# First loads and first steps laid in another order, in a windowed attention with FFN on one core

## The chip, the cores and the metric

One core of a Trainium2 chip runs the whole program. The metric is device time in microseconds, the median of several executions; the profile is of one execution and gives a span, from the first to the last instruction, which is a little less than the device time. Engines: TensorE (PE; its weight loads are PEld), VectorE (DVE), ScalarE (ACT), GpSimd (POOL) and SyncE (SP). Each works through its own queue in the order in which the program wrote it.

## The reference, cut to what matters

Batch 4, 8 heads, 768 tokens, head size 64; n_global is 8, n_local 96. A token attends to the first 8 tokens and to the 96 tokens up to itself.

```python
scores = scale * np.matmul(q, k.transpose(0, 1, 3, 2))
rel = pos[:, None] - pos[None, :]
is_global = pos[None, :] < int(n_global)
is_local = (rel >= 0) & (rel < int(n_local))
keep = is_global | is_local
dist = np.where(is_global & ~is_local, float(n_local), np.abs(rel).astype(np.float32))
scores = np.where(keep, scores - slopes[:, None, None] * dist[None], -1e9)   # softmax over the last axis
x = (softmax(scores) @ v).transpose(0, 2, 1, 3).reshape(3072, 512)
h = x @ w_in                                        # 512 x 2048
g = np.maximum(h, 0.0) + np.log1p(np.exp(-np.abs(h)))
return g @ w_out                                    # 2048 x 512, float32
```

## The kernel before, in words

The 3072 tokens are 24 blocks of 128, six to a batch. With a window of 96, a block needs the scores against itself and the block ahead of it; the 8 global tokens are copied into unused rows of the block ahead (`gk` for keys, `gv` for values). The FFN works on chunks of two blocks, 256 tokens. The heads go in two halves of four, written n.0 and n.1.

The program is a list of named steps, each a short function. Steps with a block number n:

- `l`, `lv`: loads of q and k, and of v, issued by GpSimd (line 97), 128 KB each on arrival. `load_w_in` (line 102) and `load_w_out` (line 108) bring the weights in four pieces each, 512 KB a piece.
- `t`: eight transposes on TensorE into the bank `tr` (line 208), first those of q, then those of k; VectorE copies them to QT (line 214) and KT (line 220). From block 8 on `d` does it by DMA from SP. The openings of blocks 0 and 1 have `tr_first_q` and `tr_first_k`, where k goes to a bank of its own and ScalarE copies KT of block 1.
- `s`: scores of a half, 8 matmuls (4 for the first block of a batch) into the one bank s_ps (line 258); VectorE adds the bias and gives Z (lines 270 and 272), and with it s_ps is free.
- `e`: the exponential of Z on ScalarE, giving Pb (line 294).
- `p`: Pb times v on TensorE into the one bank x_ps (line 307); VectorE takes the reciprocal of the sum (line 318) and multiplies, giving xsf (line 321).
- `x`: transposes of xsf on TensorE through the bank `tr` (line 336), copied to XT (line 339); from block 6 on by DMA.

Steps with a unit number u, eight units to a chunk: `f` is FFN in, 8 matmuls of 256 columns into one of two buffers hT (line 352), then two passes of ScalarE, an exponential (e_sb, line 357) and a logarithm (G, line 358). `o` is FFN out, 4 matmuls of 512 columns (line 372), and with every fourth a copy on VectorE and a store. Units f0 and f1 need the first piece of w_in, f2 and f3 the second, f4 and f5 the third, f6 and f7 the fourth; o0 and o4 need the first piece of w_out, o1 and o5 the second, and so on. `g` makes GpSimd wait for a G, so that later loads come when they should. `w` is a warm matmul of 512 columns on zeros, into a buffer nobody reads (line 452).

Each engine's queue is the program's order, so a step that waits holds up what stands behind it on its engine. The order comes from three places: the loads written out at the top (lines 151 to 156 and 176 to 179), the function `opening` (line 464), which handles blocks 0 and 1 with 28 warm matmuls in between, and the string `ORDER` (line 420), which goes from f0 to f27. What is not named there is sorted by due times (lines 510 to 521). Loads by GpSimd use eight semaphores in turn: a load waits until the eighth load ahead of it has landed.

Of the kernel before, what the change touches and what calls it, by code (L numbers as in the profile page):

```python
# [19 lines left out]
def kernel(  # L20
# [11 lines left out]
    nc = tc.nc  # L32
# [18 lines left out]
    NU = NFB // 2  # L51
    NWC = 4
# [23 lines left out]
    q_t = [q_r[n % RQK] for n in range(NB)]  # L76
    k_t = [k_r[n % RQK] for n in range(NB)]
    v_t = [v_r[n % RV] for n in range(NB)]
# [3 lines left out]
    q_f = const.tile([P, H, D], F32, name="q_f")  # L82
    k_f = const.tile([P, H, D], F32, name="k_f")
# [11 lines left out]
    def load(n, src, dst):  # L95
        b, i = divmod(n, BPB)
        nc.gpsimd.dma_start(  # L97
            dst[n][:, :, 0:D], src[b, :, i * P : (i + 1) * P, :].rearrange("h s d -> s h d")
        )

    def load_w_in(c):
        nc.gpsimd.dma_start(
            w_in_c[c][:],
            moe_w_in[:, c * FW : (c + 1) * FW].rearrange("(m p) f -> p m f", p=P),
        )

    def load_w_out(c):
        nc.gpsimd.dma_start(
            w_out_c[c][:],
            moe_w_out[c * FW : (c + 1) * FW, :].rearrange("(a p) c -> p a c", p=P),  # L110
        )

    def load_qk(n):
        load(n, q, q_t)
        load(n, k, k_t)

    def load_v(n):
        load(n, v, v_t)

    def load_block(n):  # L120
        load_qk(n)
        load_v(n)

    _tables = list(get_activation_tables(nc.m.arch).keys())
    nc.scalar.add_instruction(
        mybir.InstLoadActFuncSet(
            name=nc.get_next_instruction_name(),
# [20 lines left out]
        allow_small_or_imprecise_dtypes=True,  # L148
    )
    make_identity(nc, ident)  # L150
    load(1, q, q_t)
    load(1, k, k_t)
    load(0, v, v_t)
    load(1, v, v_t)
    load_w_in(0)
    load_w_in(1)

    def tables():
        nc.vector.tensor_scalar(
# [13 lines left out]
    tables()  # L173
    ones(2, RV)

    load_block(2)
    load_block(3)
    load_w_in(2)
    load_w_in(3)

    def head_of(half, r):
        return 4 * half + 2 * ((r // 2) % 2) + r // 4

    def bias_first(half):
        for r in range(0, 8, 2):
            nc.scalar.mul(bias0[:, half, r // 2, :], dist_0[:], -slopes[head_of(half, r)])

    def bias_rest(half):
        for r in range(8):
            nc.scalar.mul(  # L190
                biasA[:, half, r, :], (dist_p if r % 2 else dist_d)[:], -slopes[head_of(half, r)]
            )
# [73 lines left out]
    def add_bias(n, half):  # L266

        Z = new_Z(n, half)
        if n == first_of(n):
            nc.vector.tensor_tensor(Z[:, 0:4, :], s_ps[:, 0:8:2, :], bias0[:, half, :, :], ALU.add)  # L270
        else:
            nc.vector.tensor_tensor(Z[:], s_ps[:], biasA[:, half, :, :], ALU.add)  # L272

    def sc(n, half):

        qk(n, half, lambda r: s_ps[:, r, :])
        if n < NBT:
            add_bias(n, half)
            return
        s_lo = ps.tile([P, 4, P], F32, tag="tr", name="s_lo")  # L280
        s_hi = ps.tile([P, 4, P], F32, tag="o2", name="s_hi")
        qk(n, 1, lambda r: (s_lo if r < 4 else s_hi)[:, r % 4, :])
        add_bias(n, 0)
        step, bias = (2, bias0) if n == first_of(n) else (1, biasA)
        w = 4 // step
        Z = new_Z(n, 1)
        for i, s_i in enumerate((s_lo, s_hi)):
            regs = slice(i * w, i * w + w)
            nc.vector.tensor_tensor(Z[:, regs, :], s_i[:, 0:4:step, :], bias[:, 1, regs, :], ALU.add)  # L289

    def ex(n, half):
        nreg = 4 if n == first_of(n) else 8
        Pb = work.tile([P, 8, P], BF16, tag="Pb", name="Pb")
        nc.scalar.activation(  # L294
            Pb[:, 0:nreg, :], Zt.pop((n, half))[:, 0:nreg, :], AF.Exp, scale=inv_sqrt
        )
        Pt[n, half] = Pb

    def pv(n, half):
        first = n == first_of(n)  # L300
        Pb = Pt.pop((n, half))
        for lh in range(4):
            mm, sub = lh // 2, lh % 2
            h = 4 * half + lh
            for t in range(1 if first else 2):
                r = 2 * sub + mm if first else 4 * sub + 2 * mm + t
                nc.tensor.matmul(  # L307
                    x_ps[:, lh, :], Pb[:, r, :], v_t[n - t][:, h, :],
                    start=(t == 0), stop=(t == 1 or first),
                )  # L310
        if half == 0:
            xt[n] = (
                work.tile([P, H, D], BF16, tag="xsf", name="xsf"),
                work.tile([P, H], F32, tag="rcp", name="rcp"),
            )
        xsf, rcp = xt[n]
        h0 = 4 * half
        nc.vector.reciprocal(  # L318
            rcp[:, h0 : h0 + 4], x_ps[:, :, D : D + 1].rearrange("p h e -> p (h e)")
        )  # L320
        nc.vector.tensor_tensor(  # L321
            xsf[:, h0 : h0 + 4, :], x_ps[:, :, 0:D],
            rcp[:, h0 : h0 + 4][:, :, None].to_broadcast([P, 4, D]), ALU.mult,
        )

    def tr_x(n):
        xsf, _ = xt.pop(n)
        if n % 2 == 0:
            XT[n // 2] = xtp.tile([P, NPAIR, CT], BF16, tag="XT", name="XT")
        dst = XT[n // 2][:, :, P * (n % 2) : P * (n % 2) + P]  # L330
        if n >= NDX:
            nc.sync.dma_start_transpose(dst, xsf[:].rearrange("p h d -> p (h d)"))
            return
        tr = ps.tile([P, 2, NPAIR, P], BF16, tag="tr", name="tr")
        for m in range(NPAIR):
            nc.tensor.transpose(  # L336
                tr[:, 0, m, :], xsf[:, 2 * m : 2 * m + 2, :].rearrange("p a b -> p (a b)"), ident[:]
            )
        nc.vector.tensor_copy(dst, tr[:, 0, :, :])
# [66 lines left out]
    def gate(s):  # L406
# [3 lines left out]


    LAG = 13
    KINDS = {
        "t": tr_qk, "d": dma_qk, "gk": gk, "gv": gv, "s": sc, "e": ex, "p": pv, "x": tr_x,
        "l": load_qk, "lv": load_v, "g": gate,
    }

    ORDER = """  # L420
        f0 gv2 gk2 t2 l6 lv6 f1 s2.0 e2.0 f2 t3 l7 lv7 s2.1 e2.1 gk3 f3 p2.0 s3.0 e3.0 f4 p2.1
        gv3 s3.1 e3.1 gk4 f5 x2 p3.0 f6 t4 p3.1 f7 x3 s4.0 f8 f9 e4.0 s4.1 t5 f10 g9 l8 gk5 e4.1
        f11 gv4 o4 p4.0 o0 o1 s5.0 f12 p4.1 o5 o6 e5.0 x4 gv5 s5.1 e5.1 f13 p5.0 o2 t6 o7 p5.1
        s6.0 e6.0 o3 t7 f14 g13 l9 s6.1 d8 p6.0 e6.1 f15 x5 s7.0 o8 o9 p6.1 e7.0 s7.1 gk8 f16
        g15 lv8 d9 p7.0 x6 e7.1 o10 f17 f18 g17 l10 p7.1 f19 s8.0 x7 d10 f20 g19 lv9 e8.0 gv8
        gk9 o11 e8.1 f21 f22 g21 l11 p8.0 s9.0 o12 p8.1 o13 e9.0 gv9 o14 e9.1 f23 p9.0 f24 f25
        p9.1 x8 f26 x9 gk10 gv10 o15 f27
    """

    def steady(n):  # L430
# [5 lines left out]
            f"x{n}": s + 3.25,  # L436
        }

    def run(name):
        kind = name.rstrip("0123456789.")  # L440
        nums = [int(i) for i in name[len(kind):].split(".")]
        if kind in "fo":
            (ffn1 if kind == "f" else ffn2)(*divmod(nums[0], NU))
        else:
            KINDS[kind](*nums)

    warm_ps = ps2.tile([P, DM], F32, tag="hT", name="warm_ps")

    def warm(count):

        for _ in range(count):
            nc.tensor.matmul(warm_ps[:], warm_in[:, 0:P], warm_in[:])  # L452

    def tr_first_q(n):
        tr = qk_bank()
        tr_in(tr, 0, q_t[n])
        to_QT(n, tr)

    def tr_first_k(n):
        tr = ps.tile([P, 2, NPAIR, P], BF16, tag="o2", name="tr_k")  # L460
        tr_in(tr, 1, k_t[n])
        to_KT(n, tr, nc.vector.tensor_copy if n == 0 else nc.scalar.copy)

    def opening():

        warm(8)
        bias_first(0)
        bias_first(1)
        bias_rest(0)
        bias_rest(1)  # L470
        nc.vector.tensor_copy(q_t[0][:], q_f[:])
        nc.vector.tensor_copy(k_t[0][:], k_f[:])
        tr_first_q(0)
        warm(1)
        tr_first_k(0)
        warm(2)
        sc(0, 0)
        ex(0, 0)
        tr_first_q(1)
        tr_first_k(1)  # L480
        warm(1)
        sc(0, 1)
        ex(0, 1)
        warm(1)
        pv(0, 0)
        sc(1, 0)
        ex(1, 0)
        warm(1)
        pv(0, 1)
        warm(2)  # L490
        sc(1, 1)
        tr_x(0)
        ex(1, 1)
        warm(3)
        pv(1, 0)
        warm(5)
        pv(1, 1)
        warm(3)
        tr_x(1)
        warm(1)  # L500

    opening()
    load_block(4)
    load_block(5)
    for c in range(NWC):
        load_w_out(c)
    first_steps = ORDER.split()
    for name in first_steps:
        run(name)
# [47 lines left out]
```

## Time and profile before

| what | value |
|---|---|
| median of 3 runs | 218.59 us (218.58 to 220.5) |
| profiled execution, its own time | 218.55 us |
| its span | 216.8 us |
| TensorE busy | 210.1 us, 97% |
| ScalarE busy | 163.2 us, 75% |
| VectorE busy | 116.1 us, 54% |
| GpSimd busy | 74.0 us, 34% |
| software DMA queue, share of 16 engines | 83.8% |
| first FFN matmul (f0) | 15.86 us |

The page shows busy times and shares of the span per engine, and groups of instructions by line. A timeline line gives the start, the length, the engine, the line of the program, what is written from what, how many instructions went together, and in brackets how long the engine was idle before and what released it. TensorE's matmuls are pipelined: the length of one includes the time until its result is there, so what a step costs TensorE is read from start to start.

### The profile page before, as it was taken

The numbers are of one execution on the slowest core, as the hardware profiler recorded it, in microseconds if no ns is written. First come the engines' busy times: TensorE is split into PE (matmuls) and PEld (weight loads), VectorE is DVE, ScalarE is ACT, GpSimd is POOL, SyncE is SP. The second block draws the span as 40 slices with busy tenths as digits, with TensorE's granted clock in tenths as the row PEclk, the third lists the DMA queues.
The fourth block names the chain that finished last, engine by engine and source line by source line (L and its number), as shares of the span: only waits on it lengthen the run. The fifth ranks groups of instructions, "written<-read, shape, count | busy, mean of one in ns | idle before, by whom it ended". The sixth has DMA issues, their size and how long they took to land.

```text
span 216.8 us, 5048 instructions
## 1 busy us (share of the span) xinstructions
PE 210.1 (97%) x2004; PEld 142.3 (66%) x2004; DVE 116.1 (54%) x259; ACT 163.2 (75%) x266; POOL 74.0 (34%) x117
## 2 busy tenths in 40 slices
PE   7989899999999999999999999999999999999993
PEld 2448776666768666666677666667667667666453
DVE  6776965696674464464674674364574573011121
ACT  7737998567999979768878878868978978777200
POOL 8959473331534624424334334343311000000000
PEclk9999999999999999999999999999999999999999
DMA  9999999999999999999999999999992620111112
GB/s 129 162 178 187 172 193 206 165 161 136 124 96 168 142 167 155 136 153 102 153 102 135 152 117 124 155 146 91 170 136 41 97 73 15 60 51 48 48 48 97
DMA packets 110071, 27.06 MB, mean 125 GB/s; under 512 B 102624, under 2 KB 107104, under 8 KB 110048
## 3 DMA queue, kind: packets, MB, share of 16 engines
q0 software_dynamic: 77024, 13.37, 83.8%
q1 hardware_dynamic: 33024, 13.38, 31.8%
q8 instruction: 15, 0.25, 0.4%
q14 instruction: 8, 0.07, 0.1%
HBM read 27.26 MB, written 6.29 MB: 155 GB/s over the span
## 4 chain that ended last, share of the span: by engine, by line
PE 89%; ACT 5%; DVE 3%; DMA 1%; issue 0%; DVEq 0%
PE o L372 37%; PE hT L352 37%; PE x_ps L307 4%; PE s_ps L258 4%; PE warm_ps L452 3%; ACT Pb L294 2%; DVE Z L272 2%; ACT G L358 1%; PE s_lo L258 1%; ACT e_sb L357 1%; PE tr L208 1%; PE o L394 1%; DMA out_dram<-osb 1%; DVE Z L270 1%; PE tr L336 0%
## 5 line engine op out<-in xcount | busy, mean ns | idle before, releaser
L352 PE MATMUL hT<-XT,w_in 128*128 128x256 bf16 x768 | 98.5, 273 | 0.9 <-DMA w_in<-in_moe_w_in_dram 0.3
L372 PE MATMUL o<-w_out,G 128*128 128x512 bf16 x368 | 92.5, 379 | 0.0
L352 PEld LDWEIGHTS <-w_in 128*128 128x128 bf16 x768 | 74.0, 98 | 25.6 <-issue 0.7
L357 ACT ACTIVATE e_sb<-hT 128x512 f32<-128x512 f32 x96 | 56.5, 588 | 23.4 <-PE hT L352 22.2
L358 ACT ACTIVATE G<-e_sb 128x512 bf16<-128x512 f32 x96 | 60.5, 630 | 3.5
L294 ACT ACTIVATE Pb<-Z 128x1024 bf16<-128x1024 f32 (+1 forms) x48 | 46.6, 976 | 10.8 <-DVE Z L272 8.8
L372 PEld LDWEIGHTS <-G 128*128 128x128 bf16 x368 | 32.3, 98 | 27.3
L272 DVE TENSOR_TENSOR Z<-s_ps,biasA 128x1024 f32<-128x1024 f32 x26 | 31.8, 1223 | 10.4 <-PE s_ps L258 9.2
L318 DVE RECIPROCAL rcp<-x_ps 128x4 f32<-128x4 f32 x48 | 8.7, 180 | 49.5 <-PE x_ps L307 49.5
L378 DVE COPY osb<-o 128x512 f32<-128x512 f32 x23 | 15.7, 684 | 25.5 <-PE o L372 25.4
L409 POOL COPY gate_t<-G 1x1 bf16<-1x1 bf16 x32 | 5.7, 178 | 67.3 <-ACT G L358 67.3
L97 POOL DMA_DIRECT2D v_t<-in_v_dram x24 | 21.2, 885 | 7.4 <-PE x_ps L307 2.4
L97 POOL DMA_DIRECT2D q_t<-in_q_dram x23 | 20.5, 890 | 8.8 <-issue 4.8
L97 POOL DMA_DIRECT2D k_t<-in_k_dram x23 | 20.4, 889 | 3.5 <-PE hT L352 1.8
L321 DVE TENSOR_TENSOR xsf<-x_ps,rcp 128x256 bf16<-128x256 f32 x48 | 20.4, 424 | 1.7
L307 PEld LDWEIGHTS <-Pb 128*128 128x128 bf16 x352 | 16.7, 98 | 3.4 <-ACT Pb L294 1.2
L307 PE MATMUL x_ps<-v_t,Pb 128*128 128x65 bf16 x352 | 18.6, 193 | 0.1
L258 PEld LDWEIGHTS <-KT 64*128 64x128 bf16 x352 | 10.2, 94 | 7.6 <-issue 5.4
L258 PE MATMUL s_ps<-QT,KT 64*128 64x128 bf16 x232 | 12.1, 219 | 1.0 <-DVE Z L272 0.8
L452 PE MATMUL warm_ps<-warm_in 128*128 128x512 bf16 x28 | 10.3, 479 | 1.2 <-DVE v_t L89 1.2
L289 DVE TENSOR_TENSOR Z<-s_hi,biasA 128x512 f32<-128x512 f32 x14 | 9.5, 680 | 0.0
L289 DVE TENSOR_TENSOR Z<-s_lo,biasA 128x512 f32<-128x512 f32 x14 | 9.5, 680 | 0.0
(49 smaller groups left out, 82.7 us busy)
## 6 DMA issues: line engine op xcount, KB each, us to landing
out_dram<-osb SPq DMA_DIRECT2D x23, 256.0 KB, 3.2
v_t<-in_v_dram POOLq DMA_DIRECT2D x24, 128.0 KB, 4.5
q_t<-in_q_dram POOLq DMA_DIRECT2D x23, 128.0 KB, 4.7
k_t<-in_k_dram POOLq DMA_DIRECT2D x23, 128.0 KB, 5.0
w_in<-in_moe_w_in_dram POOLq DMA_DIRECT2D x4, 512.0 KB, 9.5
w_out<-in_moe_w_out_dram POOLq DMA_DIRECT2D x4, 512.0 KB, 10.7
XT<-xsf SPq DMA_TRANSPOSE x18, 4.1
q_f<-in_q_dram SPq DMA_DIRECT2D x1, 256.0 KB, 3.2
```

Source lines behind the costliest of these rows:

```text
L97: nc.gpsimd.dma_start(dst[n][:, :, 0:D], src[b, :, i * P : (i + 1) * P, :].rearrange("h s d -> s h d"))
L258: nc.tensor.matmul(dst(4 * sub + 2 * mm + t), KT[n - t][rows, m, :], QT[n][rows, m, :])
L272: nc.vector.tensor_tensor(Z[:], s_ps[:], biasA[:, half, :, :], ALU.add)
L289: nc.vector.tensor_tensor(Z[:, regs, :], s_i[:, 0:4:step, :], bias[:, 1, regs, :], ALU.add)
L294: nc.scalar.activation(Pb[:, 0:nreg, :], Zt.pop((n, half))[:, 0:nreg, :], AF.Exp, scale=inv_sqrt)
L307: nc.tensor.matmul(x_ps[:, lh, :], Pb[:, r, :], v_t[n - t][:, h, :], start=(t == 0), stop=(t == 1 or first),)
L321: nc.vector.tensor_tensor(xsf[:, h0 : h0 + 4, :], x_ps[:, :, 0:D], rcp[:, h0 : h0 + 4][:, :, None].to_broadcast([P, 4, D]), ALU.mult,)
L352: nc.tensor.matmul(hT[:, j, :], w_in_c[wc][:, m, fo : fo + P], XT[c][:, m, :], start=(m == 0), stop=(m == KM - 1),)
L357: nc.scalar.activation(e_sb[:], hT[:], AF.Exp)
L358: nc.scalar.activation(G[c][:, 2 * u : 2 * u + 2, :], e_sb[:], AF.Ln, bias=1.0)
L372: nc.tensor.matmul(o[:], G[c][:, 4 * kq + a, ns * P : ns * P + P], w_out_c[kq][:, a, :], start=(kq == 0 and a == 0), stop=(kq == NWC - 1 a ...
L452: nc.tensor.matmul(warm_ps[:], warm_in[:, 0:P], warm_in[:])
```

## The change

The first loads stand in another order: q and k of blocks 2 and 3 (tokens 256 to 511) come ahead of w_in, and v of blocks 2 and 3 in between the first two pieces of w_in. The third and fourth piece of w_in, the pieces of w_out and the loads of blocks 4 and 5 are now steps within the order. The function `opening` is gone; its steps stand in the string, with t2, t3, both halves of s2 and s3.0 ahead of f0, and 26 warm matmuls. The other steps up to f27 are the same, laid in a new order; after f27 nothing differs.

```diff
-    load(1, q, q_t)
-    load(1, k, k_t)
-    load(0, v, v_t)
-    load(1, v, v_t)
-    load_w_in(0)
-    load_w_in(1)
+    load_qk(1)
+    load_v(0)
+    load_v(1)
+    load_qk(2)
+    load_qk(3)
...
-    load_block(2)
-    load_block(3)
-    load_w_in(2)
-    load_w_in(3)
+    load_w_in(0)
+    load_v(2)
+    load_w_in(1)
+    load_v(3)
...
     ORDER = """
-        f0 gv2 gk2 t2 l6 lv6 f1 s2.0 e2.0 f2 t3 l7 lv7 s2.1 e2.1 gk3 f3 p2.0 s3.0 e3.0 f4 p2.1
-        gv3 s3.1 e3.1 gk4 f5 x2 p3.0 f6 t4 p3.1 f7 x3 s4.0 f8 f9 e4.0 s4.1 t5 f10 g9 l8 gk5 e4.1
-        f11 gv4 o4 p4.0 o0 o1 s5.0 f12 p4.1 o5 o6 e5.0 x4 gv5 s5.1 e5.1 f13 p5.0 o2 t6 o7 p5.1
...
+        w8 b0 bb1 cq0 ck0 tq0 w1 tk0 w2 s0.0 b1 tq1 bb0 tk1 w1 e0.0 s0.1 e0.1
+        l4 wi2 wi3 wo0 l5 lv4 wo1 lv5 wo2 wo3
+        w2 p0.0 s1.0 t2 l6 lv6 p0.1 e1.0 w1 s1.1 gk2 e1.1 w2 x0 p1.0 w2 s2.0 t3 l7 lv7 e2.0 p1.1
+        w2 s2.1 e2.1 gk3 w2 x1 gv2 w3 s3.0
+        f0 p2.0 f1 s3.1 e3.0 p2.1 e3.1 f2 gv3 t4 gk4 f3 p3.0 x2 s4.0 p3.1 f4 f5 s4.1 x3 f6 gk5
+        f7 f8 o4 f9 t5 e4.0 o0 f10 g9 l8 s5.0 e4.1 f11 o5 f12 gv4 p4.0 s5.1 o1 e5.0 p4.1 f13 gv5
+        e5.1 f14 g13 l9 x4 p5.0 o2 o3 p5.1 t6 o6 f15 s6.0 e6.0 x5 o7 s6.1 t7 e6.1 p6.0 f16 g15
...
     """
...
-    def opening():
-
-        warm(8)
-        bias_first(0)
-        bias_first(1)
-        bias_rest(0)
-        bias_rest(1)
-        nc.vector.tensor_copy(q_t[0][:], q_f[:])
-        nc.vector.tensor_copy(k_t[0][:], k_f[:])
-        tr_first_q(0)
-        warm(1)
-        tr_first_k(0)
-        warm(2)
-        sc(0, 0)
-        ex(0, 0)
-        tr_first_q(1)
-        tr_first_k(1)
-        warm(1)
-        sc(0, 1)
-        ex(0, 1)
-        warm(1)
-        pv(0, 0)
-        sc(1, 0)
-        ex(1, 0)
-        warm(1)
-        pv(0, 1)
-        warm(2)
-        sc(1, 1)
-        tr_x(0)
-        ex(1, 1)
-        warm(3)
-        pv(1, 0)
-        warm(5)
-        pv(1, 1)
-        warm(3)
-        tr_x(1)
-        warm(1)
-
-    opening()
-    load_block(4)
-    load_block(5)
-    for c in range(NWC):
-        load_w_out(c)
```

In the new string `b` and `bb` are the ScalarE passes that build the bias tables, `cq` and `ck` the casts of block 0, `tq` and `tk` the first transposes, `wi` and `wo` the weight pieces.

More of the change, by code (lines that the diff above doesn't have):

```diff
@@ L118, in load_v @@
         load(n, v, v_t)
-    def load_block(n):
-        load_qk(n)
-        load_v(n)
     _tables = list(get_activation_tables(nc.m.arch).keys())
@@ L412 @@
     LAG = 13
[L413 to L416, printed above, removed]
     ORDER = """
-        f0 gv2 gk2 t2 l6 lv6 f1 s2.0 e2.0 f2 t3 l7 lv7 s2.1 e2.1 gk3 f3 p2.0 s3.0 e3.0 f4 p2.1
-        gv3 s3.1 e3.1 gk4 f5 x2 p3.0 f6 t4 p3.1 f7 x3 s4.0 f8 f9 e4.0 s4.1 t5 f10 g9 l8 gk5 e4.1
-        f11 gv4 o4 p4.0 o0 o1 s5.0 f12 p4.1 o5 o6 e5.0 x4 gv5 s5.1 e5.1 f13 p5.0 o2 t6 o7 p5.1
[L424 to L427, printed above, removed]
+        w8 b0 bb1 cq0 ck0 tq0 w1 tk0 w2 s0.0 b1 tq1 bb0 tk1 w1 e0.0 s0.1 e0.1
[5 more added lines that the diff above has]
+        e5.1 f14 g13 l9 x4 p5.0 o2 o3 p5.1 t6 o6 f15 s6.0 e6.0 x5 o7 s6.1 t7 e6.1 p6.0 f16 g15
+        lv8 f17 s7.0 o8 e7.0 d8 p6.1 f18 g17 l10 s7.1 d9 e7.1 f19 p7.0 o9 f20 g19 lv9 p7.1 o10 gk8
+        gv8 f21 s8.0 x6 e8.0 gk9 f22 g21 l11 o11 e8.1 f23 p8.0 x7 d10 s9.0 o12 o13 p8.1 gk10 o14
+        gv9 e9.0 e9.1 f24 p9.0 x8 f25 p9.1 f26 x9 gv10 o15 f27
     """
@@ L437, in steady @@
         }
[L439 to L445, printed above, removed]
     warm_ps = ps2.tile([P, DM], F32, tag="hT", name="warm_ps")
@@ L452, in warm, with cast_q, cast_k @@
             nc.tensor.matmul(warm_ps[:], warm_in[:, 0:P], warm_in[:])
+    def cast_q(n):
+        nc.vector.tensor_copy(q_t[n][:], q_f[:])
+    def cast_k(n):
+        nc.vector.tensor_copy(k_t[n][:], k_f[:])
     def tr_first_q(n):
@@ L462, in tr_first_k, with run @@
         to_KT(n, tr, nc.vector.tensor_copy if n == 0 else nc.scalar.copy)
-    def opening():
-        warm(8)
-        bias_first(0)
-        bias_first(1)
-        bias_rest(0)
-        bias_rest(1)
-        nc.vector.tensor_copy(q_t[0][:], q_f[:])
-        nc.vector.tensor_copy(k_t[0][:], k_f[:])
-        tr_first_q(0)
-        warm(1)
-        tr_first_k(0)
-        warm(2)
-        sc(0, 0)
-        ex(0, 0)
-        tr_first_q(1)
-        tr_first_k(1)
-        warm(1)
-        sc(0, 1)
-        ex(0, 1)
-        warm(1)
-        pv(0, 0)
-        sc(1, 0)
-        ex(1, 0)
-        warm(1)
-        pv(0, 1)
-        warm(2)
-        sc(1, 1)
-        tr_x(0)
-        ex(1, 1)
-        warm(3)
-        pv(1, 0)
-        warm(5)
-        pv(1, 1)
-        warm(3)
-        tr_x(1)
-        warm(1)
-    opening()
-    load_block(4)
-    load_block(5)
-    for c in range(NWC):
-        load_w_out(c)
+    KINDS = {
+        "t": tr_qk, "d": dma_qk, "gk": gk, "gv": gv, "s": sc, "e": ex, "p": pv, "x": tr_x,
+        "l": load_qk, "lv": load_v, "g": gate, "w": warm, "b": bias_first, "bb": bias_rest,
+        "cq": cast_q, "ck": cast_k, "tq": tr_first_q, "tk": tr_first_k,
+        "wi": load_w_in, "wo": load_w_out,
+    }
+    def run(name):
+        kind = name.rstrip("0123456789.")
+        nums = [int(i) for i in name[len(kind):].split(".")]
+        if kind in "fo":
+            (ffn1 if kind == "f" else ffn2)(*divmod(nums[0], NU))
+        else:
+            KINDS[kind](*nums)
     first_steps = ORDER.split()
```

## The prediction, made before the changed kernel had run

> **What bounds the kernel now.** I read the page first: TensorE is busy nearly all the span, so only time it spends on fillers or waiting can be won.
>
> ```profile
> PE 210.1 (97%) x2004; PEld 142.3 (66%) x2004; DVE 116.1 (54%) x259; ACT 163.2 (75%) x266; POOL 74.0 (34%) x117
> ...
> L452 PE MATMUL warm_ps<-warm_in 128*128 128x512 bf16 x28 | 10.3, 479 | 1.2 <-DVE v_t L89 1.2
> ```
>
> The 28 warm_ps matmuls compute nothing. Next, TensorE's timeline over the first 30 us: start, length, and how many went together.
>
> ```profile
> 9.91 0.30 PE L307 MATMUL x_ps<-v_t,Pb 128*128 128x65 bf16 x4
> ...
> 11.03 0.40 PE L258 MATMUL s_ps<-QT,KT 64*128 64x128 bf16 x8 [0.39 <-DVE Z L272]
> ...
> 12.35 0.41 PE L307 MATMUL x_ps<-v_t,Pb 128*128 128x65 bf16 x8
> 12.59 1.24 PE L452 MATMUL warm_ps<-warm_in 128*128 128x512 bf16 x5
> ...
> 15.86 1.03 PE L352 MATMUL hT<-XT,w_in 128*128 128x256 bf16 x8 [0.30 <-DVE XT L339]
> 16.73 0.39 PE L208 MATMUL tr<-ident,q_t 128*128 128x128 bf16 x4
> 16.95 0.39 PE L208 MATMUL tr<-ident,k_t 128*128 128x128 bf16 x4
> 17.17 1.04 PE L352 MATMUL hT<-XT,w_in 128*128 128x256 bf16 x8
> 18.18 0.40 PE L258 MATMUL s_ps<-QT,KT 64*128 64x128 bf16 x8
> 18.51 1.05 PE L352 MATMUL hT<-XT,w_in 128*128 128x256 bf16 x8
> ...
> 22.73 1.05 PE L352 MATMUL hT<-XT,w_in 128*128 128x256 bf16 x8 [0.34 <-DMA w_in<-in_moe_w_in_dram]
> ...
> 29.60 0.61 PE L352 MATMUL hT<-XT,w_in 128*128 128x256 bf16 x4 [0.19 <-ACT G L358]
> ```
>
> What a step costs TensorE is the distance between starts: f 0.87 (15.86 to 16.73), t 0.44 (16.73 to 17.17), s 0.33 (18.18 to 18.51), p 0.24 (12.35 to 12.59); x is 0.22 and a warm matmul 0.21 in the same way. FFN begins at 15.86 (f0); f4 waits for w_in at 22.73; f8 begins at 29.60.
>
> The timeline of GpSimd tells when loads land, since a ninth load waits for the first of the eight before it:
>
> ```profile
> 12.43 0.76 POOL L102 DMA_DIRECT2D w_in<-in_moe_w_in_dram  x1 [0.44 <-DMA w_in<-in_moe_w_in_dram]
> 14.97 0.74 POOL L102 DMA_DIRECT2D w_in<-in_moe_w_in_dram  x1 [1.78 <-DMA w_in<-in_moe_w_in_dram]
> ...
> 22.96 0.75 POOL L108 DMA_DIRECT2D w_out<-in_moe_w_out_dram  x1 [1.02 <-DMA w_in<-in_moe_w_in_dram]
> ```
>
> These are w_in 0, 1 and 2 landed. A weight piece takes 14.97 - 12.43 = 2.54; from w_in 1 to w_in 2 there are six q, k, v blocks and one piece in 7.99, so a block takes (7.99 - 2.54)/6 = 0.91. TensorE saw w_in 2 at 22.73, so it sees a landing 0.23 before these rows.
>
> Last, the chain of waits between f1 and f8 runs over ScalarE:
>
> ```profile
> 19.95 1.06 ACT Pb L294
> 21.01 0.49 ACT e_sb L357
> 21.53 0.63 ACT G L358
> 22.16 0.95 ACT Pb L294
> ```
>
> An f costs ScalarE 0.49 + 0.63 = 1.12 against 0.87 on TensorE, an exp of scores 0.95. Before f0 ScalarE stood idle 3.08 (ahead of the e_sb at 16.93).
>
> **The change part by part.** Both orders hold the same steps up to f27, and behind f27 nothing is changed; so the gain is what TensorE loses less up to there.
>
> Warm matmuls go from 28 to 26: 2 x 0.21 = 0.43 at most, all of it ahead of f0 where TensorE waits anyway; it is inside the times below.
>
> Loads. q and k of blocks 2 and 3 go ahead of w_in 0, which moves four issues (0.87 to 0.95 each on GpSimd, ending near 9) down that queue; GpSimd stays far ahead of the transfers, so issue costs nothing and the transfers' order decides. v 1 lands 2.54 before w_in 0: 12.43 - 2.54 - 0.23 = 9.66 for TensorE. Then q2 10.57, k2 11.48, q3 12.4, k3 13.3, w_in 0 15.8 (12.2 before), v2 16.7, w_in 1 19.3, v3 20.2, q4 21.1, k4 22.0, w_in 2 24.5, w_in 3 27.1, w_out 0 29.6, k5 31.4, v4 32.4, w_out 1 34.9, w_out 2 38.3. The total is the same, so blocks 6 on land when they did. SP's queue has nothing until d8, far behind.
>
> The opening. Up to s0.1 (8.10) nothing moves. The copy of KT 1 goes ahead of e0.0 on ScalarE: 0.54 later (8.08 to 8.62), so p0.0 moves from 8.77 to about 9.0; s1.0 waited for Z of s0.1 till 9.24 and stays. Now the new wait: t2 stands ahead of p0.1 in TensorE's queue, and its k half cannot run before 11.5. Behind it wait p0.1 (ran at 9.91, now 11.74) and s1.1 (11.03, now 12.07); on VectorE, behind the copies QT2 and KT2, the division of p0.1 and Z of s1.1. VectorE then runs without a gap, at the distances of its own timeline:
>
> ```profile
> 9.75 1.22 DVE L272 TENSOR_TENSOR Z<-s_ps,biasA 128x1024 f32<-128x1024 f32 x1
> 10.89 0.17 DVE L318 RECIPROCAL rcp<-x_ps 128x4 f32<-128x4 f32 x1
> 11.10 0.42 DVE L321 TENSOR_TENSOR xsf<-x_ps,rcp 128x256 bf16<-128x256 f32 x1
> 11.53 1.23 DVE L272 TENSOR_TENSOR Z<-s_ps,biasA 128x1024 f32<-128x1024 f32 x1
> ```
>
> Z takes 1.14 of VectorE, rcp and xsf together 0.64; QT and KT copies are 0.34 each (17.37 and 17.71), XT 0.33, gk 0.1. From 11.94: QT2, KT2, xsf 0.1, Z1.1 (starts 13.2), gk, XT, xsf 1.0, Z2.0 (15.3), QT3, KT3, xsf 1.1, Z2.1 (17.6), XT at 18.84, done 19.26. TensorE follows: s2.0 at 14.5, s2.1 16.5, s3.0 19.0, f0 at 19.31.
>
> Of the 3.45 by which f0 is later, t2, t3 (0.88) and s2.0, s2.1, s3.0 (1.0) are work brought forward: 1.88. Loss: 1.57.
>
> From f0 to f8. Before: 13.74 for 8 f, 3 t, 5 s, 4 p, 2 x = 6.98 + 1.33 + 1.66 + 0.96 + 0.45 = 11.38; lost 2.36, to ScalarE and w_in. After: ScalarE has e2.0 and e2.1 behind it in what was its idle time. From the e_sb of f0 at 20.4 it runs F0, F1, e3.0, e3.1, F2 to F5 and half of F6: 6.5 x 1.12 + 2 x 0.95, and hT is free for f8 at 29.6 to 29.9. I take 29.85. By then TensorE has done s4.1 as well: 8 f, 1 t, 3 s, 4 p, 2 x = 9.83 of 10.54, lost 0.71. Gain 1.65.
>
> Every weight piece comes in time, if narrowly: f2 at 21.9 (w_in 1 19.3), f4 25.5 (24.5), f6 27.9 (27.1), o4 30.7 (29.6), t5 32.5 (31.4), o5 35.9 (34.9). From f8 to f27 I find no wait that differs.
>
> Sum: 1.57 - 1.65 = -0.08. The same stepping through, done for the order of before, puts f8 at 30.00 where the row has 29.60; its error of 0.4 would be in my 29.85 too, and I take off somewhat more than half of it: -0.35. Bounds of the one new price, k2's landing: q4 and k4 landed 1.67 behind w_in 3 (rows 25.54 and the k half of t4 at 26.98, less 0.23 at POOL), 0.84 each, and v 1 could be seen a block earlier; at the other end half a weight piece each, 1.27, k2 at 12.2. Everything up to f8 moves with it one for one: -0.9 to +0.7. I take 0.91, the mean of six such loads.
>
> The profiled run took 218.55 for a span of 216.8; 218.55 - 0.35 = 218.2. The median, 218.59, is 0.04 above it.
>
> [...] Warm matmuls start 0.43 apart until 7 us (weight loads at 2.02, 2.45, 2.87) and 0.21 later, so TensorE runs at half speed first and a gap might bring that back. After the change TensorE streams only about 1.1 in the 3.4 us from 8.2 to 11.6 (w2, p0.0, s1.0, half of t2), about 1.6 in the 2.9 before 11.03 in the old order. [...]
>
> **The rivals.** Early loads: v 1's block of delay doesn't recur, k2 lands near 10.6, f0 at 18.4, 0.9 less: 217.3. For it: GpSimd issued k2 at 6.1. Against: each landing row fits one steady stream.
>
> Late loads, the other side: q2 and k2 land over 0.35 later than I take (k2 past 11.85) and hold p0.1, s1.1 and all behind them. At 1.27 a block, +0.7: 218.9; each 0.5 more costs 0.5, and the margins of 0.8 to 1.1 at f4 to o5 go too.
>
> [...]
>
> No loss at f8 and early loads at once (ScalarE holds nothing): -0.9 - 0.7 - 0.35, 216.6, about 0.9%.
>
> **How the numbers follow.** Forecast 0.47 (217.7 to 218.7), early loads 0.17, late loads 0.19 (to about 221), clock 0.09 (to 221.8), no loss 0.08. Within 1%, 216.4 to 220.8, is no change, about what a measurement of this kernel can tell. Faster: 0.05, some half of the last case, whose 216.6 lies close to the bound. Slower: 0.10, half of the clock case and a quarter of the late loads. Same: 0.85. The range 216.9 to 219.8 leaves out most of "no loss", a third of the late loads and half of the clock: 0.06 + 0.06 + 0.05 = 0.17.
>
> **What would show it.** Right: t2's k half near 11.5 with a DMA wait ahead of it, p0.1 behind it, f0 near 19.3, no DMA wait at f4, f6 or o4, f8 near 29.7, f27 ending within 1 us of before's 69.5. Wrong: p0.1 before 11; 512-column warm matmuls 0.43 apart past 8 us; a wait for w_in or w_out of over 0.5.

## The result, and the profile after

The changed kernel took 220.7 us (median of 19 runs, 219.52 to 223.43) against 218.95 for the kernel before (19 runs, 218.43 to 220.5). The ratio is 1.0077, with a 95% interval of 1.0059 to 1.0095: slower, by less than 1%. That is 2.5 us over the predicted 218.2 and 0.9 over the upper end of the range. The profiled execution took 222.89 us, with a span of 221.1 and a mean granted clock of 0.992. The 19 runs fall into two groups, which matters below: 8 with a mean clock of 0.991 or 0.992 took 221.61 to 223.43, 11 with 0.997 or more 219.52 to 221.72. The ratio leaves the four longest runs out, the profiled one among them.

From the page of the changed kernel, the line of the engines and two groups of matmuls (busy time and mean ns of one; then idle time ahead of them, and what ended most of it):

```profile
PE 211.0 (95%) x2002; PEld 142.4 (64%) x2002; DVE 116.1 (53%) x259; ACT 163.7 (74%) x266; POOL 73.8 (33%) x117
...
L347 PE MATMUL hT<-XT,w_in 128*128 128x256 bf16 x768 | 99.9, 275 | 2.6 <-DMA XT<-xsf 2.6
L367 PE MATMUL o<-w_out,G 128*128 128x512 bf16 x368 | 92.8, 379 | 0.6 <-DMA w_out<-in_moe_w_out_dram 0.6
```

TensorE's share fell from 97% to 95%. FFN in lost 2.6 us to a DMA that writes XT, FFN out 0.6 us to w_out. TensorE's timeline of the changed kernel says where:

```profile
10.22 0.40 PE L203 MATMUL tr<-ident,k_t 128*128 128x128 bf16 x4 [0.42 <-DMA k_t<-in_k_dram]
10.46 0.29 PE L302 MATMUL x_ps<-v_t,Pb 128*128 128x65 bf16 x4
...
18.24 1.03 PE L347 MATMUL hT<-XT,w_in 128*128 128x256 bf16 x8
...
27.47 2.79 PE L347 MATMUL hT<-XT,w_in 128*128 128x256 bf16 x24
30.84 1.02 PE L367 MATMUL o<-w_out,G 128*128 128x512 bf16 x4 [0.58 <-DMA w_out<-in_moe_w_out_dram]
...
63.71 1.03 PE L367 MATMUL o<-w_out,G 128*128 128x512 bf16 x4
67.33 1.87 PE L347 MATMUL hT<-XT,w_in 128*128 128x256 bf16 x8 [2.60 <-DMA XT<-xsf]
68.99 0.65 PE L302 MATMUL x_ps<-v_t,Pb 128*128 128x65 bf16 x8
69.45 1.67 PE L347 MATMUL hT<-XT,w_in 128*128 128x256 bf16 x8
70.96 0.41 PE L302 MATMUL x_ps<-v_t,Pb 128*128 128x65 bf16 x8
```

The k half of t2 starts at 10.22 with p0.1 behind it; f0 is at 18.24. The three f from 27.47 put f8 at 27.47 + 2 x 0.87 = 29.21. o4 waits 0.58 for the first piece of w_out. At 67.33 stands f24, the first f of the chunk of blocks 6 and 7, after 2.60 of idling; then an f takes 1.66 (67.33 to 68.99) instead of 0.87 us, and a p 0.46 instead of 0.24. In the kernel before, f24 and f25 run without a wait:

```profile
64.90 1.91 PE L352 MATMUL hT<-XT,w_in 128*128 128x256 bf16 x16
```

The windows of the changed kernel give the reason (length; busy time and count of PE, PEld, DVE, ACT, POOL; granted clock, DMA share, GB/s):

```profile
67.40:70.70 3.30, 3.30 (x22) 2.46 (x23) 0.61 (x2) 1.23 (x2) 0.00 (x0) 0.50 0.68 94
70.80:74.00 3.20, 3.20 (x33) 2.52 (x32) 1.49 (x4) 2.34 (x4) 1.12 (x3) 1.00 0.20 41
```

The granted clock is 0.50 for the first stretch behind the wait and 1.00 after it.

Why XT was late is read on the queue of SP, which issues the DMA transposes. The changed kernel:

```profile
55.15 1.26 SPq L327 DMA_TRANSPOSE XT<-xsf  x1
61.30 0.34 SPq L375 DMA_DIRECT2D out_dram<-osb  x1
61.69 2.58 SPq L327 DMA_TRANSPOSE XT<-xsf  x1
64.37 1.21 SPq L227 DMA_TRANSPOSE QT<-q_t  x1
```

and the kernel before, around the same two steps:

```profile
54.44 2.65 SPq L332 DMA_TRANSPOSE XT<-xsf  x2
60.13 1.19 SPq L232 DMA_TRANSPOSE QT<-q_t  x1
```

Before, x6 and x7 went out one behind the other, at 54.44 and 55.9. In the changed string x7 stands behind o11 ("x6 e8.0 gk9 f22 g21 l11 o11 e8.1 f23 p8.0 x7"), and o11 ends with a store that SP issues. SP issues in that order: the store goes out at 61.30, with its data, and the transpose of x7 behind it at 61.69. VectorE of the changed kernel shows which of the two was ready when:

```profile
56.25 0.42 DVE L316 TENSOR_TENSOR xsf<-x_ps,rcp 128x256 bf16<-128x256 f32 x1
...
58.18 1.23 DVE L267 TENSOR_TENSOR Z<-s_ps,biasA 128x1024 f32<-128x1024 f32 x1 [1.23 <-PE s_ps L253]
59.32 0.68 DVE L284 TENSOR_TENSOR Z<-s_lo,biasA 128x512 f32<-128x512 f32 x1
59.92 0.68 DVE L284 TENSOR_TENSOR Z<-s_hi,biasA 128x512 f32<-128x512 f32 x1
...
60.59 0.68 DVE L373 COPY osb<-o 128x512 f32<-128x512 f32 x1
```

The last xsf of block 7 is done at 56.67, 5 us before its transpose is issued. The copy that the store needs stands behind three passes for Z on VectorE and is done at 61.27. The chain of waits of the changed kernel runs through exactly this:

```profile
60.84 0.43 DVE osb L373
...
61.69 5.51 DMA XT<-xsf
67.20 0.14 issue
67.33 1.87 PE hT L347 x8
```

From issue to landing the transpose took 5.51 us; the same one took 3.3 in the kernel before.

The sum, from start to start: f8 at 29.21 is 0.64 ahead of my 29.85, which stood for -0.08, so -0.72. o4 could have started at 29.21 + 0.87 = 30.08 and starts at 30.84: +0.76. The wait at f24 (o14 is through at 63.71 + 0.86 = 64.57) costs 67.33 - 64.57 = 2.76. At half clock f24, p9.0, f25 and p9.1 start later by what they take too long: 71.20 - 67.33 = 3.87 for two f and two p of 2.22, so 1.65. Together +4.45, where the spans differ by 221.1 - 216.8 = 4.3. The 0.15 between them is the kernel before's: from f8 to f24 it takes 64.90 - 29.60 = 35.30, of which s4.1 and p9.0 (0.57) stand elsewhere in the new order, so 34.73 against 67.33 - 29.21 - 0.76 - 2.76 = 34.60.

This sum is of the profiled execution alone. The median is 1.75 over the kernel before's, and the 11 runs without the lower clock have a median of 220.18, 1.2 over it. An estimate from that, if the other terms (-0.72, 0.76 and -0.15) are the same: f24 waits some 1.3 us in those, not 2.76. No trace shows one of them.

### The profile page after: what moved, and what is told of

The parts are those of the page before. It is cut to its first block, busy times and chain, and to the rows that moved or that the text cites. A ratio compares the mean times of both kernels' runs of the same rounds, so it can differ in the third digit from the quotient of the medians.

```text
span 221.1 us, 5046 instructions
## 1 busy us (share of the span) xinstructions
PE 211.0 (95%) x2002; PEld 142.4 (64%) x2002; DVE 116.1 (53%) x259; ACT 163.7 (74%) x266; POOL 73.8 (33%) x117
## 4 chain that ended last, share of the span: by engine, by line
PE 80%; DMA 13%; POOL 3%; DVE 1%; issue 1%; SPq 0%; POOLq 0%; DVEq 0%
PE o L367 35%; PE hT L347 35%; DMA w_out<-in_moe_w_out_dram 6%; PE x_ps L302 4%; DMA w_in<-in_moe_w_in_dram 3%; PE s_ps L253 3%; DMA XT<-xsf 2%; PE s_lo L253 1%; POOL q_t L97 1%; POOL k_t L97 1%; PE o L389 1%; POOL v_t L97 1%; DMA out_dram<-osb 1%; PE tr L203 1%; DVE Z L284 1%
## 5 line engine op out<-in xcount | busy, mean ns | idle before, releaser
L347 PE MATMUL hT<-XT,w_in 128*128 128x256 bf16 x768 | 99.9, 275 | 2.6 <-DMA XT<-xsf 2.6
L347 PEld LDWEIGHTS <-w_in 128*128 128x128 bf16 x768 | 74.8, 99 | 28.4 <-issue 3.1
L267 DVE TENSOR_TENSOR Z<-s_ps,biasA 128x1024 f32<-128x1024 f32 x26 | 31.7, 1221 | 11.3 <-PE s_ps L253 10.6
L438 PE MATMUL warm_ps<-warm_in 128*128 128x512 bf16 x26 | 9.4, 467 | 1.2 <-DVE v_t L89 1.2
```

Source lines behind the costliest of these rows:

```text
L347: nc.tensor.matmul(hT[:, j, :], w_in_c[wc][:, m, fo : fo + P], XT[c][:, m, :], start=(m == 0), stop=(m == KM - 1),)
```

## The experiments

The theory: x7 behind o11's store costs the 2.8 us of waiting and, in some runs, the 1.65 at half clock; without it the change is what was predicted, a few tenths. The first rival: the opening or the waits between f8 and f24 cost it. The second: the landing time of the transpose, not its place in the queue, is to blame. Ratios are to the kernel before, run beside each version on the same chip.

**x7_front**: the changed kernel with x7 ahead of o11.

```diff
-        gv8 f21 s8.0 x6 e8.0 gk9 f22 g21 l11 o11 e8.1 f23 p8.0 x7 d10 s9.0 o12 o13 p8.1 gk10 o14
+        gv8 f21 s8.0 x6 x7 e8.0 gk9 f22 g21 l11 o11 e8.1 f23 p8.0 d10 s9.0 o12 o13 p8.1 gk10 o14
```

> The changed kernel with one step moved: x7 stands right behind x6, ahead of the store of o11 in SP's queue. Theory (x7 sits behind that store, its transpose lands at 67.2 and f24 waits 2.6 us): x7 is issued before 58, f24 starts near 64.6 with no DMA wait, clock 1.000 in every run, span 216.4 to 217.2, ratio to before 0.997 to 1.002. Rival (the opening and the loads lose the time, f24's wait only shows slack used up): the time stays at 219.5 or more, ratio 1.004 or more. Rival (another wait takes its place, d10 or x8 being later): in between, with a new DMA wait in the 20 us behind f24.

Measured: 218.54 us (217.62 to 219.48, 12 runs), ratio 0.9986 (0.9966 to 1.0005). SP and TensorE of this kernel:

```profile
55.42 3.09 SPq L327 DMA_TRANSPOSE XT<-xsf  x2
61.90 0.34 SPq L375 DMA_DIRECT2D out_dram<-osb  x1
```

```profile
22.88 0.40 PE L203 MATMUL tr<-ident,q_t 128*128 128x128 bf16 x4 [0.65 <-DMA q_t<-in_q_dram]
23.77 0.40 PE L203 MATMUL tr<-ident,k_t 128*128 128x128 bf16 x4 [0.50 <-DMA k_t<-in_k_dram]
...
65.17 1.04 PE L347 MATMUL hT<-XT,w_in 128*128 128x256 bf16 x8
```

Both transposes go out one behind the other (x7 at 57.3), f24 waits for no DMA, and the store, as late as before, holds up nothing that matters. One step's place carries the whole loss, some 0.9% of the time. My "clock 1.000 in every run" did not hold: six of the twelve have it, five have 0.997 or 0.998, the profiled one among them (0.998 over a span of 217.3), and one, of 218.22 us, has 0.990, which no trace explains. The profiled execution, 219.09, is among the longer ones: there t4 waited 1.15 in all for q and k of block 4; in the changed kernel's it waited 0.25, for k alone. So the loads of the opening came about 1 us apart in these two executions, with the same order of loads.

**store_act**: x7 stays where the change put it, but the store of o11 is issued from ScalarE's queue.

```diff
-            nc.sync.dma_start(out[n0 : n0 + P, :], osb[:])
+            (nc.scalar if (c, ns) == (1, 0) else nc.sync).dma_start(out[n0 : n0 + P, :], osb[:])
```

> The changed kernel with x7 left where it is, but the store of o11 issued from ScalarE's queue, so that nothing waits ahead of x7 on SP but x6 and d9. Theory (it is the store, waiting for VectorE's osb copy, that holds x7): x7 issued before 59, no wait at f24, time within 0.5 us of the run with x7 in front; ScalarE may lose up to 1 us waiting for the copy, off the path. Rival (x7's own place behind p8.0 or its slow landing does it): f24 still waits over 1.5 us and the time stays near 220.2.

Measured: 217.59 us (217.5 to 218.04, 6 runs), ratio 0.995 (0.9934 to 0.9965). SP of this kernel, then ScalarE's queue:

```profile
54.08 2.81 SPq L327 DMA_TRANSPOSE XT<-xsf  x2
57.00 1.21 SPq L227 DMA_TRANSPOSE QT<-q_t  x1
```

```profile
60.29 0.37 ACTq L375 DMA_DIRECT2D out_dram<-osb  x1
```

x7 goes out right behind x6, at 55.7, though it stands behind o11 in the program, whose store goes at 60.29; it is the wait of the store in SP's queue that held it in the changed kernel. This version is 0.5% ahead of the kernel before, and 0.95 us ahead of x7_front, where I had expected 0.5 at most. It also gets the transposes of d10 out early, from 57.00 (62.34 in x7_front). But in the two profiles the difference lies ahead of f8 (28.81 against 30.57, behind the late loads of block 4); from f8 to f24 they take 34.75 and 34.60.

**before_store_act**: the same edit in the kernel before, as a control for whether it is worth something by itself.

> The kernel before with the store of o11 issued from ScalarE's queue, a control for the same edit in the changed kernel. Theory (that edit pays there only because x7 stood behind the store; here x7 goes ahead of it): ratio 0.999 to 1.001. Rival (the edit is worth 0.3% or more by itself, through d10 or x8 or the DMA queues): ratio under 0.998.

Measured: 219.35 us (218.75 to 220.46, 12 runs), ratio 1.0019 (1.0004 to 1.0034). Nothing gained, a little lost; the interval lies somewhat above what was expected. What store_act gained is not the edit as such.

**before_x7_late**: the kernel before with x7 put behind its o11, so that the suspected cost comes without the rest of the change.

```diff
-        g15 lv8 d9 p7.0 x6 e7.1 o10 f17 f18 g17 l10 p7.1 f19 s8.0 x7 d10 f20 g19 lv9 e8.0 gv8
-        gk9 o11 e8.1 f21 f22 g21 l11 p8.0 s9.0 o12 p8.1 o13 e9.0 gv9 o14 e9.1 f23 p9.0 f24 f25
+        g15 lv8 d9 p7.0 x6 e7.1 o10 f17 f18 g17 l10 p7.1 f19 s8.0 d10 f20 g19 lv9 e8.0 gv8
+        gk9 o11 e8.1 f21 f22 g21 l11 p8.0 x7 s9.0 o12 p8.1 o13 e9.0 gv9 o14 e9.1 f23 p9.0 f24 f25
```

> The kernel before with x7 alone moved behind the store of o11 (and behind p8.0), as the change has it; opening and loads untouched. Theory: the store goes at about 60.0 (osb copy 59.33 + 0.67), x7 at 60.4, landing 2.4 to 5.5 later (62.8 to 65.9) against f24 at 63.95: 0 to 2.0 us more, most likely 0.5 to 1.5, ratio 1.001 to 1.009, with a wait of f24 for XT. Rival (x7's place doesn't matter, the loss needs the new opening): ratio 0.998 to 1.001 and no such wait.

Measured: 225.84 us (224.06 to 226.91, 6 runs), ratio 1.0313 (1.0278 to 1.0348). SP, TensorE and a window of this kernel:

```profile
60.32 1.20 SPq L232 DMA_TRANSPOSE QT<-q_t  x1
61.69 1.77 SPq L233 DMA_TRANSPOSE KT<-k_t  x1
63.56 0.53 SPq L380 DMA_DIRECT2D out_dram<-osb  x1
64.14 11.49 SPq L332 DMA_TRANSPOSE XT<-xsf  x3
```

```profile
69.72 3.57 PE L352 MATMUL hT<-XT,w_in 128*128 128x256 bf16 x16 [3.98 <-DMA XT<-xsf]
```

```profile
68.30:75.00 6.70, 5.28 (x31) 3.81 (x32) 1.30 (x5) 2.45 (x4) 0.18 (x1) 0.50 0.60 51
```

The direction holds, but the size is far over what I expected. I had not seen that here d10 stands ahead of the store: the store goes out at 63.56 (63.38 in the kernel before), x7 at 64.14, and what I had as f24's place, 63.95, was f23's. The wait is 3.98, and half clock lasts over 6.7 us, twice as long as in the changed kernel.

**fill**: the changed kernel with 12 matmuls on zeros (into a buffer that nobody reads) in the gap ahead of f24, to part the half clock from the wait.

```diff
-        gv9 e9.0 e9.1 f24 p9.0 x8 f25 p9.1 f26 x9 gv10 o15 f27
+        gv9 e9.0 e9.1 wf12 f24 p9.0 x8 f25 p9.1 f26 x9 gv10 o15 f27
```

> The changed kernel with 12 more warm matmuls (2.6 us at 0.21) ahead of f24, so that TensorE streams while x7 is under way; nothing else moves. Theory (the half clock after f24, matmuls 0.21 apart where they were 0.11, comes from the idle wait): f24 starts where it did, 66 to 67.5, then at full speed; no run with a mean clock below 0.997; median near 220.1, ratio 1.004 to 1.009. Rival (the half clock has nothing to do with the wait): runs at clock 0.992 and 222 us stay in about the same share, 8 of 19.

Measured: 221.78 us (220.14 to 223.32, 6 runs), ratio 1.0143 (1.0104 to 1.0182). TensorE and a window of this kernel:

```profile
64.03 2.75 PE L443 MATMUL fill_ps<-warm_in 128*128 128x512 bf16 x12
66.62 1.04 PE L347 MATMUL hT<-XT,w_in 128*128 128x256 bf16 x8
```

```profile
66.70:70.00 3.30, 3.25 (x42) 2.89 (x42) 1.41 (x5) 2.25 (x4) 0.00 (x0) 1.00 0.68 91
```

In the profile the reading holds: f24 starts as long after o14 (2.59, against 2.76; x7, issued at 61.15, landed after 5.2, at about 66.4, and the matmuls on zeros end just ahead of f24), and behind the filled gap the clock is 1.00 and an f takes 0.87 (66.62 to 67.49). None of the six runs is at 0.992, but one, at 0.994, lies below the 0.997 I had named. The time misses the expectation: 220.64 for the profiled execution, but a median of 221.78. Why four of the other runs took 0.9 to 2.7 us more isn't shown. A part may be that the matmuls on zeros hold f24 for their 2.6 us in every run, also where x7 has landed earlier.

**l11_late**: x7 stays behind the store, but q and k of block 11 are loaded later, away from its transpose.

```diff
-        gv8 f21 s8.0 x6 e8.0 gk9 f22 g21 l11 o11 e8.1 f23 p8.0 x7 d10 s9.0 o12 o13 p8.1 gk10 o14
+        gv8 f21 s8.0 x6 e8.0 gk9 f22 o11 e8.1 f23 p8.0 x7 d10 s9.0 o12 o13 g23 l11 p8.1 gk10 o14
```

> The changed kernel with x7 where it is, behind the store; only the loads of q11 and k11 on GpSimd go later, gated by G of f23 in place of f21. Theory (x7's transpose took 5.5 us from issue to landing because it shares the DMA engines with those loads, against 2.1 where x7 goes early): issued near 61.5, landed by 64.5, f24 waits under 0.5 us, ratio 0.996 to 1.002. Rival (the late issue behind the store is enough, or the store itself slows it): landing still 4 us or more after issue, f24 waits over 1.5, ratio 1.004 or more.

Measured: 219.49 us (218.02 to 220.33, 12 runs), ratio 1.0003 (0.9977 to 1.0029). SP and TensorE of this kernel:

```profile
61.71 2.41 SPq L327 DMA_TRANSPOSE XT<-xsf  x1
```

```profile
65.52 1.03 PE L347 MATMUL hT<-XT,w_in 128*128 128x256 bf16 x8 [0.77 <-DMA XT<-xsf]
66.39 0.41 PE L302 MATMUL x_ps<-v_t,Pb 128*128 128x65 bf16 x8
```

x7 is issued at 61.71, just as late, but lands after 3.7 us, at about 65.4, instead of 5.51. That is later than the 64.5 I had expected; the 2.1 that I gave for an early x7 was wrong too, it took 3.5 in x7_front. The wait shrinks from 2.60 to 0.77 and half clock doesn't follow (f24 takes 0.87). So the second rival is half right: the late issue uses up all the slack, and the slower landing beside the loads makes a wait of 0.8 into one of 2.6.

**loads_only**: the kernel before with the new order of loads alone.

> The kernel before, its steps untouched, with the changed kernel's order of loads alone. Theory (the new order pays only with the new steps): TensorE gets w_in 0 to 3 at about 16.2, 19.8, 24.9 and 27.4, where f0, f2, f4 and f6 ran at 15.86, 18.51, 22.73 and 25.73; f0 to f6 wait for w_in, some 1.5 to 2.2 us more in all, ratio 1.006 to 1.011. Rival (ScalarE bounds that stretch and hides the later pieces): at most 0.5 us, ratio under 1.003.

Measured: 221.01 us (220.73 to 221.48, 6 runs), ratio 1.0095 (1.0077 to 1.0113), as expected. f0, f2 and, with 1.22 us, f4 wait for w_in; f6 doesn't. TensorE:

```profile
16.51 1.05 PE L351 MATMUL hT<-XT,w_in 128*128 128x256 bf16 x8 [1.20 <-DMA w_in<-in_moe_w_in_dram]
...
20.58 1.05 PE L351 MATMUL hT<-XT,w_in 128*128 128x256 bf16 x8 [1.33 <-DMA w_in<-in_moe_w_in_dram]
```

With the old steps FFN comes too early for its weights.

**steps_only**: the new steps (with x7 in front) and the old order of loads.

> The changed kernel's steps with x7 in front, but the loads in the order of before. Theory (the new steps need the new loads): t2's k half waits for k2 until about 16.5 with p0.1 and s1.1 behind it, f0 near 24, ratio 1.02 to 1.03. Rival (the steps alone bring the gain and the loads' order is indifferent): ratio under 1.002.

Measured: 225.05 us (224.49 to 225.74, 6 runs), ratio 1.0269 (1.024 to 1.0298). TensorE and a window:

```profile
16.73 0.61 PE L205 MATMUL tr<-ident,q_t 128*128 128x128 bf16 x4 [7.25 <-DMA q_t<-in_q_dram]
...
26.73 1.03 PE L349 MATMUL hT<-XT,w_in 128*128 128x256 bf16 x8
```

```profile
12.80:22.90 10.10, 5.94 (x49) 3.43 (x50) 3.78 (x10) 1.06 (x1) 6.77 (x8) 0.50 1.84 180
```

t2 waits 7.25 for q of block 2, and within the wait a stretch of 10 us at half clock begins, which I had not counted: f0 is at 26.73, not near 24. Loads and steps of this change pay only together: 0.95% lost with the one, 2.7% with the other, nothing or a little gained with both (x7_front).

**x7_o4**: x7_front, and o4 behind f9, for the 0.58 that o4 waited.

```diff
-        f7 f8 o4 f9 t5 e4.0 o0 f10 g9 l8 s5.0 e4.1 f11 o5 f12 gv4 p4.0 s5.1 o1 e5.0 p4.1 f13 gv5
+        f7 f8 f9 o4 t5 e4.0 o0 f10 g9 l8 s5.0 e4.1 f11 o5 f12 gv4 p4.0 s5.1 o1 e5.0 p4.1 f13 gv5
```

> The changed kernel with x7 in front, and o4 behind f9 as well. Theory (o4 at 30.1 stands ahead of w_out 0, which lands between 29.4 and 30.8): its wait goes, 0 to 0.7 us less than with x7 in front alone, ratio 0.994 to 0.999. Rival (f9 then waits for its hT buffer, which ScalarE holds): the DMA wait at o4 turns into an equal wait at f9, time as with x7 in front.

Measured: 218.09 us (217.84 to 218.55, 8 runs), ratio 0.9959 (0.9944 to 0.9974). TensorE:

```profile
27.56 3.91 PE L347 MATMUL hT<-XT,w_in 128*128 128x256 bf16 x32
31.31 1.03 PE L367 MATMUL o<-w_out,G 128*128 128x512 bf16 x4
```

No wait ahead of o4 is left; the four f ahead of it take 3.75 (27.56 to 31.31) instead of 3.48, so 0.27 of it went to them. x7_front's profile had no wait at o4 either, since its f8 came late, and the two ratios' intervals overlap: what moving o4 is worth isn't shown.

**both_o4**: x7_o4 with the store of o11 on ScalarE's queue as well.

> The changed kernel with x7 in front, o4 behind f9, and the store of o11 on ScalarE's queue: the version to beat both. Theory: no DMA wait over 0.3 us from f8 on; ratio 0.992 to 0.997, like the run with the store on ScalarE alone or a little less. Rival (loads that land 0.8 us late on one DMA engine set the time, whatever the order of the later steps): ratio 0.996 to 1.000, with waits at f2, t4 or f4.

Measured: 218.38 us (217.81 to 218.73, 11 runs), ratio 0.996 (0.9941 to 0.9979), with no wait of TensorE for a DMA from f8 to f24: the two cures don't add up. With x7 in front, the store holds up d10, and x7_front's profile has no wait of TensorE for that.

**x7_o4_p0**: x7_o4 with p0.1 ahead of t2, out of the wait for k of block 2.

```diff
-        w2 p0.0 s1.0 t2 l6 lv6 p0.1 e1.0 w1 s1.1 gk2 e1.1 w2 x0 p1.0 w2 s2.0 t3 l7 lv7 e2.0 p1.1
+        w2 p0.0 s1.0 p0.1 t2 l6 lv6 e1.0 w1 s1.1 gk2 e1.1 w2 x0 p1.0 w2 s2.0 t3 l7 lv7 e2.0 p1.1
```

> As the run with x7 in front and o4 behind f9, and p0.1 ahead of t2 on TensorE as well. Theory (t2 waits 0.6 to 1.1 for q2 and k2 with p0.1 behind it, and VectorE's division of p0.1 behind QT2 and KT2): s1.1 and f0 some 0.3 to 0.6 earlier, ratio 0.002 below the run with o4 alone. Rival (VectorE runs without a gap from there on and the order of its work changes nothing at f0): f0 within 0.2 of 18.4, ratio within 0.0015 of that run's 0.9959.

Measured: 218.19 us (217.62 to 219.34, 12 runs), ratio 0.9958 (0.9934 to 0.9982). p0.1 runs at 9.88, f0 at 18.24 against 18.39 in x7_o4. p0.1 wasn't the brake; VectorE's row of passes, the rival, sets f0.

## Why the prediction was wrong, step by step

**The step that failed** is in one sentence: "From f8 to f27 I find no wait that differs." I followed TensorE, ScalarE and the loads there, and of SP I wrote that its "queue has nothing until d8, far behind". That is true for the opening and is no answer for what comes after it. The order of SP's queue around x7, the store of o11 and d10 had changed, and a transpose that had gone out with its data at 56 went out at 61.69. Its own time, 3.3 to 5.5 us from issue to landing, was never priced, so its slack wasn't either. The wait it made, put at nothing in my sum, was 2.76 us in the profiled execution, with another 1.65 of half clock behind it. Undoing that one move (x7_front) or its cause alone (store_act) takes the loss away.

**The clock rival** had half clock in the opening, where it didn't come: from 8.2 to f0 the granted clock was 1.00, and in the stretch from 8.2 to 11.6 TensorE was busy for 2.77 of the 3.40 us (each matmul counted until its result is there). Half clock came behind the wait of f24, at 67.34, where no rival had put it, held for 3.4 us and cost 1.65. No run shows the term behind the 221.8 that the chances give this rival; the changed kernel's trace showed those 3.4 us in its place, and steps_only's, with the old order of loads, 10.2 us from within a wait of 7.25.

**The loads** came as in the rival of early loads, not as in the forecast: the k half of t2 ran at 10.22, not 11.5 (rival: about 10.6), f0 at 18.24, not 19.31 (rival: 18.4). In x7_front's profile q and k of block 4 came late. That is not the rival of late loads, which had k of block 2 past 11.85: there too t2's k half ran at 10.72.

**The margin of o4** was given as 1.1 (needed at 30.7, landed at 29.6). Measured: needed at 30.08, landed at 30.8, so a loss of 0.76, of which the page shows 0.58 as idle. TensorE was earlier by 0.6 and the load later by 1.2. That is the sign I named as wrong, a wait for w_out of over 0.5; the other margins held.

**What was right:** the order of the opening with VectorE as its limit (x7_o4_p0), no waits at f4 and f6, f8 within 0.64 of where it was put. That ScalarE keeps the gain to tenths isn't shown: it was busy for 10.1 of the 11.0 us from f0 to f8, but the waits of TensorE there were for k of block 4 and for VectorE. The sum of -0.35 us is a ratio of 0.9984; x7_front, the change without its side effect, measured 0.9986, with an interval of 0.9966 to 1.0005. That agreement is partly luck. In the profile of the changed kernel the opening lost 18.24 - 15.86 - 1.88 = 0.50, not 1.57, and from f0 to f8 the gain was 2.36 - (29.21 - 18.24 - 9.83) = 1.22, not 1.65; with the wait at o4 these are errors of opposite sign.

**The best versions**, store_act at 0.995 and x7_o4 at 0.9959, are ahead of both kernels.

**Open:** why fill's median lies 1.1 above its profiled execution; and why half clock follows the wait at f24 in 8 of 19 runs only. That the runs at a mean clock of 0.992 are those with half clock at f24 is seen in the one profiled and inferred for the rest. A shorter wait in the others, as in the estimate above (some 1.3 us), would do it; that isn't shown.

## What to carry to other kernels

When steps are laid anew, write out the new order of every queue that issues DMAs, stores included, and ask of each entry what stands ahead of it and when that one's data is ready; here the store that went out on SP at 61.30 held the transpose behind it, whose data was there at 56.67, until 61.69. Give each DMA on the way to the bounding engine its measured time from issue to landing, with and without other loads beside it (5.51 and 3.7 for x7), before calling it hidden. A wait of TensorE may cost more than itself: look at the granted clock behind it (2.76 us of waiting had 1.65 from a clock of 0.50 behind it here).

## What the runs showed of the hardware

Three traces show a longer stretch of half clock. By windows of 0.2 us the granted clock was 0.50 from 67.34 to 70.75 in the changed kernel (3.4 us), from 68.21 to 75.04 in before_x7_late (6.8) and from 12.72 to 22.96 in steps_only (10.2). It set in 2.6, 2.5 and 3.2 us after the last matmul had ended (64.74, 65.74 and 9.47), in the latter two while TensorE still waited. Ahead of it, at a clock of 1.00, TensorE was busy for 0.14 of the 2.70 us from 64.60, for 0.24 of the 2.70 from 65.50, and not at all in the 3.20 from 9.50. It didn't follow the wait of 0.77 us in l11_late (1.00 from 64 to 70), nor those of 1.20 and 1.33 in loads_only (a mean clock of 1.000), nor the same gap as in the changed kernel filled with matmuls (fill: busy for 2.60 of 2.60 us from 64.00, then 1.00 from 66.7 to 74). How long or how empty a gap has to be for half clock to follow isn't shown.

One and the same DMA transpose of x7 took 3.3 to 3.7 us from issue to landing in the kernel before, x7_front, store_act and l11_late, and 5.2 to 5.5 in fill, before_x7_late and the changed kernel. Moving two loads away from it (l11_late) gave 1.8 back, from 5.51 to 3.7.

With the store on ScalarE's queue (store_act) the ratio went from 1.0077 to 0.995. What was saved was the wait of the store in SP's queue: in the changed kernel SP had issued x6 by 56.41 and issued nothing more until the store went out at 61.30, some 4.9 us.
